# Loading value pairs, query weights and mixer input weights by one transfer of 56 to 64 KB per partition instead of two

## Chip, cores and metric

The kernel runs on one core of one Trainium2 chip. The metric is device time in microseconds (us); the lower the better. A measured time is the median of a few executions. A profile is one more execution, and its *span* is 1.3 to 1.4 us shorter than the measured time of the same execution. Times inside a profile are counted from the start of its span.

## What is computed

One decode step of attention with a cache of 65,536 positions, mixed by a gate with a small gated MLP. The inputs are bf16.

```python
q = x @ wq                                # 32 heads of 128, from a row of 1024
scores = q · k_cache * Dh**-0.5           # 4 kv heads, 65,536 keys each, 8 q heads per kv head
o = softmax(scores) · v_cache
a = o @ wo
z = gelu(B_x @ w_in); z1, z2 = halves     # 1024 -> 3584
b = (z1 * (w_sp * layernorm(z2) + b_sp)) @ w_out
out = g * a + (1 - g) * b                 # g = sigmoid(sum(x * gate_w))
```

The two caches are 67 MB each, the weights some 28 MB: 162 MB must be read once, for little arithmetic.

## The kernel before

Everything that is loaded goes through one list, `stream`, in a fixed order. A block of K or V is 16,384 positions of one head group: 4 MB, 32 KB in each of 128 partitions. The K blocks use a ring of three slots. The value blocks come in pairs, and there is **one** pair buffer, `VB`, which the query and mixer weights use before.

```python
SUB = 16384                               # elements of bf16: 32 KB per partition
...
load([("wq", 0)], rows(A_wq, 0, 8), VB)
load_k(0)
load_k(1)
load([("win", 0)], rows(B_w_in, 0, 8), VB)
load_k(2)
load_k(3)
load([("wout", 0)], rows(B_w_out, 0, 14), VB)
for i in range(6):
    load_k(2 * i + 4)
    load_v2(2 * i)                        # one pair: v(2i), v(2i+1), into VB
    load_k(2 * i + 5)
load_v2(12)
load([("v", 14)], kv(A_v_cache, 14), kring())
load([("v", 15)], kv(A_v_cache, 15), kring())
# ... then the output weights wo
```

`issue()` turns list entries into transfers. A transfer is recorded as soon as the program's order allows, and on the chip it waits until the readers of the slots that it overwrites are done. Every transfer has its own completion semaphore, and a reader waits for the transfers that wrote its slots.

```python
def issue():
    while issued[0] < len(stream):
        ...
        for c in range(0, w, SUB):        # at most 32 KB per partition in one transfer
            m = min(SUB, w - c)
            P("SP", lambda e, ...: e.dma_start(arena[:, o:o + m], src),
              w=[("slot", x) for x in grains(off + c, m)], dma="s%d" % grains(off + c, m)[0])
        issued[0] += 1
...
def pv_piece(n):                          # value product n, TensorE
    sl, keys = use(("v", n))              # keys: the slots of v(n) alone
    ...
    P("PE", f, r=[("ptsb", n % 2)] + keys, w=["ob"])
    done(("v", n))                        # frees the slots of v(n); issues what can be issued
```

The main loop scores K block `2i+4`, then does the two value products `2i` and `2i+1`, then scores K block `2i+5`. The query projection (`wqs, keys = use(("wq", 0))`) and the mixer projection name the slots of the whole tensor, so both halves must have landed before their first matmul.

## Time and profile before

| | before |
|---|---|
| measured time | 383.79 us (383.66 to 383.85, 3 runs) |
| span of the profile | 382.3 us |
| moved | 162 MB, 424 GB/s over the span |
| PE / DVE busy | 61% / 55% |

From the profile page of the kernel before: the DMA and clock rows of the table of 40 slices (each digit is tenths of a slice), the packet total, and the row of the main DMA queue with its packets, its MB and its share of 16 engines' span.

```profile
PEclk9996998689979599959898998786979988778695
DMA  9999999999999999999999999999999999999995
GB/s 384 439 435 425 423 417 435 439 436 433 439 425 418 432 430 439 439 432 432 429 420 429 435 439 434 429 435 426 422 432 437 435 432 429 439 425 420 423 425 220
DMA packets 6246, 162.16 MB, mean 424 GB/s; under 512 B 728, under 2 KB 732, under 8 KB 988
q1 hardware_dynamic: 6200, 162.01, 98.8%
```

The DMA engines were busy for nine tenths or more of every slice but the last. The kernel is bound by its stream of transfers. No computing engine can make it faster.

The end of the main loop: this is TensorE's timeline there, then the issues on the SP queue in the same stretch (columns: start, duration, engine, line, operation; in brackets, the idle time before and what ended it). `obt` is written by the value products: the first `scp` row ends the score block before, the next row is the start of product 10, the row with the bracket the start of product 11.

```profile
305.29 0.38 PE L248 MATMUL scp<-arena 128*128 128x512 bf16 x1
305.60 0.41 PE L246 MATMUL obt<-arena 128*64 128x512 bf16 x2
...
308.86 0.38 PE L248 MATMUL obt<-arena 128*64 128x512 bf16 x2
311.40 0.41 PE L246 MATMUL obt<-arena 128*64 128x512 bf16 x2 [2.16 <-DMA arena<-in_A_v_cache_dram]
...
316.32 0.41 PE L248 MATMUL obt<-arena 128*64 128x512 bf16 x2
```

```profile
309.28 8.77 SPq L365 DMA_DIRECT2D arena<-in_A_v_cache_dram  x4
```

Product 10 ran at once, on the half of the pair that had long landed. Its end released half of the pair buffer, and at 309.28 the next value transfer was in the queue. Product 11 waited for its half until 311.40.

The last view of before is the list of waits: how long TensorE waited for value blocks in all, how often, and the longest.

```profile
PE obt L246 <- DMA arena<-in_A_v_cache_dram: 12.4, 5, 6.1
```

### The profile page before, as it was taken

The page shows a single profiled execution, that of the slowest core. Times are in us where ns is not written, and L with a number is a line of the kernel's source. Part 1 is how long each engine was busy: PE and PEld are TensorE (multiplying, and loading weights), DVE is VectorE, ACT ScalarE, POOL GpSimd, SP SyncE. Part 2 cuts the span into 40 slices and gives each one's busy share as a digit, 9 for nine tenths or more (in the row PEclk, how much of TensorE's full clock was granted, in tenths as well). Part 3 has the DMA queues.
Part 4 walks back from the last instruction along what each step waited for, and adds up shares of the span by engine and source line. Part 5 has one row for each costly group of instructions (what it writes and reads, how often), then busy time and mean ns, then how long its engine had stood idle before and what let it go on. Part 6 is the DMA issues. An engine that isn't in the chain of part 4 may idle for free.

```text
span 382.3 us, 2522 instructions
## 1 busy us (share of the span) xinstructions
PE 234.6 (61%) x1375; PEld 56.9 (15%) x785; DVE 211.7 (55%) x229; ACT 25.3 (7%) x39; POOL 1.5 (0%) x8
## 2 busy tenths in 40 slices
PE   0055754286687578545793777377938673849344
PEld 0011111111121111101120112012201121112121
DVE  6116952785781698067935980579448914842020
ACT  1000000102030001000210010001200100031000
POOL 1000000000000000000000000000000000000000
PEclk9996998689979599959898998786979988778695
DMA  9999999999999999999999999999999999999995
GB/s 384 439 435 425 423 417 435 439 436 433 439 425 418 432 430 439 439 432 432 429 420 429 435 439 434 429 435 426 422 432 437 435 432 429 439 425 420 423 425 220
DMA packets 6246, 162.16 MB, mean 424 GB/s; under 512 B 728, under 2 KB 732, under 8 KB 988
## 3 DMA queue, kind: packets, MB, share of 16 engines
q1 hardware_dynamic: 6200, 162.01, 98.8%
q8 instruction: 8, 0.13, 0.1%
q14 instruction: 2, 0.02, 0.0%
q10 hardware_dynamic: 36, 0.00, 0.0%
HBM read 162.01 MB, written 0.00 MB: 424 GB/s over the span
## 4 chain that ended last, share of the span: by engine, by line
DMA 61%; PE 19%; DVE 18%; SPq 1%; ACT 1%; issue 1%
DMA arena<-in_A_k_cache_dram 33%; DVE arena L476 13%; DMA arena<-in_B_w_in_dram 8%; DMA arena<-in_A_wo_dram 7%; DMA arena<-in_B_w_out_dram 6%; PE obt L246 6%; DMA arena<-in_A_wq_dram 6%; PE obt L248 5%; PE scp L246 4%; PE scp L248 4%; DVE arena L493 1%; SPq L365 1%; DVE arena L514 1%; DVE arena L464 1%; DVE arena L549 0%
## 5 line engine op out<-in xcount | busy, mean ns | idle before, releaser
L476 DVE STREAM_TRANSPOSE arena<-arena 128x2048 f32<-128x2048 f32 x64 | 145.5, 2295 | 84.5 <-DMA arena<-in_A_k_cache_dram 71.9
L246 PE MATMUL scp<-arena 128*128 128x512 bf16 x256 | 112.5, 439 | 83.4 <-DVE arena L476 61.0
L248 PE MATMUL scp<-arena 128*128 128x512 bf16 x256 | 111.0, 434 | 0.0
L246 PE MATMUL obt<-arena 128*64 128x512 bf16 (+2 forms) x334 | 64.6, 428 | 30.6 <-DMA arena<-in_A_v_cache_dram 12.4
L248 PE MATMUL obt<-arena 128*64 128x512 bf16 (+2 forms) x334 | 64.1, 424 | 0.0
L246 PEld LDWEIGHTS scp<-arena 128*128 128x128 bf16 x256 | 27.5, 107 | 192.2 <-DVE arena L476 93.8
L509 ACT ACTIVATE arena<-arena 128x1024 bf16<-128x1024 f32 x16 | 18.4, 1148 | 237.5 <-DVE arena L505 127.4
L246 PEld LDWEIGHTS obt<-arena 128*64 128x64 bf16 (+1 forms) x334 | 19.4, 116 | 86.6 <-issue 79.1
L493 DVE TENSOR_SCALAR_CACHE_REDUCE arena<-scp 128x1024 f32<-128x1024 f32 x16 | 19.3, 1205 | 9.3 <-PE scp L248 9.3
L514 DVE STREAM_TRANSPOSE arena<-arena 128x1024 bf16<-128x1024 bf16 x16 | 19.4, 1214 | 9.0 <-PE obt L248 6.4
L706 PE MATMUL fbt<-arena 128*1 128x256 bf16 x128 | 6.2, 339 | 5.9 <-DMA arena<-in_A_wo_dram 5.7
L539 DVE RECIPROCAL arena<-mbt 128x1 f32<-128x1 f32 x4 | 0.6, 139 | 14.0 <-PE mbt L535 14.0
L441 DVE CAST arena<-obt 97x1024 bf16<-97x1024 f32 x1 | 1.2, 1224 | 11.5 <-PE obt L248 11.5
L712 DVE CAST arena<-fbt 97x256 bf16<-97x256 f32 x1 | 0.4, 425 | 11.3 <-PE fbt L706 11.3
L588 DVE COPY arena<-obt 128x896 f32<-128x896 f32 x1 | 1.1, 1093 | 9.1 <-PE obt L248 9.1
L464 DVE COPY arena<-arena 32x32 bf16<-32x32 bf16 x16 | 2.7, 166 | 6.2 <-PE scp L248 6.0
L407 PE MATMUL scp<-arena 8*128 8x1 bf16 x8 | 0.6, 197 | 8.4 <-DVE arena L402 8.4
L706 PEld LDWEIGHTS fbt<-arena 128*1 128x1 bf16 x128 | 2.8, 93 | 8.8 <-DMA arena<-in_A_wo_dram 6.7
L595 ACT ACTIVATE arena<-arena 128x28 f32<-128x28 f32 x1 | 0.2, 226 | 52.4 <-DVE arena L594 52.4
L549 DVE SCALAR_TENSOR_TENSOR arena<-obt,arena 128x512 bf16<-128x512 f32 x4 | 3.0, 751 | 0.1
L601 PE MATMUL mbt<-arena 128*128 128x1 f32 x2 | 0.4, 260 | 4.3 <-DVE arena L600 4.3
L509 ACT ACTIVATION_READ_ACCUMULATOR arena<-arena 128x1 f32 x16 | 3.0, 186 | 0.0
(88 smaller groups left out, 47.0 us busy)
## 6 DMA issues: line engine op xcount, KB each, us to landing
arena<-in_A_k_cache_dram SPq DMA_DIRECT2D x16, 4096.0 KB, 38.4
arena<-in_A_v_cache_dram SPq DMA_DIRECT2D x16, 4096.0 KB, 31.1
arena<-in_A_wq_dram SPq DMA_DIRECT2D x2, 4096.0 KB, 16.8
arena<-in_A_wo_dram SPq DMA_DIRECT2D x3, 2048.0 KB, 22.6
arena<-in_B_w_in_dram SPq DMA_DIRECT2D x1, 4096.0 KB, 25.2
arena<-in_B_w_out_dram SPq DMA_DIRECT2D x1, 3584.0 KB, 23.1
arena<-in_B_w_in_dram SPq DMA_DIRECT2D x1, 3072.0 KB, 32.2
arena<-in_A_wo_dram SPq DMA_DIRECT2D x1, 1024.0 KB, 26.5
```

The source lines that it names most:

```text
L246: return e.matmul(*a, **kw)
L248: one = e.matmul(*a, **kw).ins
L365: P("SP", lambda e, o=OFF["RING"] + off + c, m=m, src=src[:, c:c + m]: e.dma_start(arena[:, o:o + m], src), w=[("slot", x) for x in grains ...
L441: P("DVE", lambda e: e.tensor_copy(psb[0:97, :], ob[0:97, :]), w=["psb", "ob"])
L464: P("DVE", lambda e, pb=pb: e.tensor_copy(vw(qpad, 24 + 32 * pb, [[QP, 4], [1, 8]], 32 * pb, 32), vw(qall, 8 * g, [[32, 4], [1, 8]], 32 * ...
L476: P("DVE", lambda e: e.transpose(ktb(i).bitcast(F32), sl[:, 4096 * p:4096 * (p + 1)].bitcast(F32)), r=keys[2 * p:2 * p + 2], w=[("kt", i % ...
L493: P("DVE", lambda e: e.tensor_scalar(scs(n), sc_ps(n), 0.0, None, op0=ALU.add, op1=ALU.max, accum_out=maxc[:, n:n + 1]), w=[("sc", n % NSC ...
L509: P("ACT", lambda e: e.activation(psb, scs(n), ACTF.Exp, bias=gcol(n // NP, K_NB), scale=SCALE, accum_out=lp[:, n:n + 1]), r=[("sc", n % N ...
L514: P("DVE", lambda e: e.transpose(ptsb(n), psb), r=["psb"], w=[("ptsb", n % 2)])
L549: P("DVE", lambda e: e.scalar_tensor_tensor(osc, ob[:, 512:1024], gcol(g, K_FB), osc, op0=ALU.mult, op1=ALU.add), r=[("fh", g, 1), "psb"], ...
L588: P("DVE", lambda e: e.tensor_copy(vw(zr, 0, [[FB4, 2], [32, FC], [1, 32]]), vw(ob, 0, [[512, 2], [1, FC], [FC, 32]])), w=[KZR, "ob"])
L706: ins = e.matmul(fb[32 * q:32 * q + 1, 0:QW], ovec[:, 8 * i + c:8 * i + c + 1], sl[:, o:o + QW], start=False, stop=(i == 3 and c == 7), ti ...
```

## The change

The intent: fewer and larger transfers, so fewer packets with their fixed costs, and fewer semaphores. The Trainium skill points in this direction in "DMA: Bandwidth & Descriptors", section "Rules for kernel authors": for full bandwidth use 128 partitions and at least 1 MiB per transfer, and coalesce small transfers. Here the transfers were already 3 to 4 MB.

```diff
-            for c in range(0, w, SUB):
-                m = min(SUB, w - c)
+            for c in range(0, w, 2 * SUB):
+                m = min(2 * SUB, w - c)
```

Seven value pairs, the query weights (64 KB per partition) and the mixer input weights (56 KB) become one transfer each. The order of instructions on PE, DVE, ACT and POOL does not change.

## The prediction

> **What bounds the kernel now.** The DMA stream. In the slice table the 16 DMA engines read 9 tenths or more in every slice but the last; the hardware queue's packets fill 98.8% of 16 engines' span, 162 MB at a mean of 424 GB/s. In the packet records the engines are never idle together from the first packet (1.0 us after the first issue) to 379.1 us of the 382.3 us span. PE (61%) and DVE (55%) have room. So only two things can change the time: how long packets take, and whether the queue runs dry.
>
> **Packets (removed).** A 4 KB packet takes 159 ns, 8 KB 312, 16 KB 614, 32 KB 1216: about 37.6 ns per KB plus 10 to 12 ns per packet. The Trainium skill ("DMA: Bandwidth & Descriptors", "Why small descriptors are slow") names such a fixed cost per packet; at 32 KB the trace leaves 1% of it. The change merges nine pairs of transfers (query weights, mixer input weights, seven value pairs), each saving 8 packets per engine: 72 x 11 ns = 0.8 us, an estimate from those durations, with 64 KB packets of about 2.42 us.
>
> **Landings (moved).** Instruction order on PE, DVE and ACT is the same. The query and mixer projections already wait for both halves before their first matmul, so their merges move nothing. The value products do change: each waited for its half; the first of a pair will wait for the whole 8 MB, some 9.7 us later. Both products then run back to back, and the next value pair, which reuses the single pair buffer, is issued after both (before, its first half went after the first product).
>
> For most pairs that is harmless: two K blocks (19.5 us of work) stand in the queue behind the pair. Pair (2,3) would be released some 3 us later than 159.4 us, with the queue filled until 175.0. Pairs (4,5) and (8,9) hardly move.
>
> **The one place on the critical path**: pair (10,11) lands at 311.3 us and only block K15 is queued behind it, done at 318.9 (first engine) to 321.0 (last). Before, product 10 ran from 305.6 to 309.2 and released half the pair at 309.3, so the queue never ran dry. After, product 10 starts at about 310.7. A product takes 3.5 us at full granted clock, and 5.2 as product 11 ran at 311.4, because PE is granted half clock after idling. I expect both to end near 320 us, and first packets 1.0 to 1.2 us after the issue (the first issue of the trace shows 1.0), at about 321.1. The slowest engine would have gone on at 320.2: a bubble of about 1 us on it, 2 to 3 us on the others. Everything behind (last value blocks, output weights, tail of 2.8 us) shifts with it but has slack: the output weights are issued 10 us before the queue ends.
>
> **Sum**: -0.8 + 1.0 = +0.2 us: predicted 384.0 us, range 382.9 to 386.0. Chances: faster by over 2% 0.02, within 2% 0.94, slower by over 2% 0.04.
>
> **Right or wrong in the profile**: 64 KB packets near 2.42 us and 1,152 fewer data packets; PE waiting longer for the value cache; no first product before its pair lands; one dip of the DMA share near 320 us and none elsewhere; last output weights landing within 1.5 us of 379.5.
>
> **What would make it wrong**: large packets slower, or split into small ones; full PE clock after pair (10,11) (no bubble, about 383.1) or half clock throughout (3 us more); another pair running the queue dry; the late value pair delaying the final products past the output weights.

## The result, and the profile after

| | before | after |
|---|---|---|
| measured time | 383.80 us (4 runs) | 386.91 us (386.25 to 387.32, 4 runs) |
| ratio | | 1.0082, 95% interval 1.0067 to 1.0096 |
| span | 382.3 us | 386.0 us |
| PE's waits for value blocks | 12.4 us | 35.2 us |

A ratio is the mean time of one kernel's fast runs over that of the other's of the same rounds, so it is not quite the ratio of the medians above. The change costs 0.8%: within 2%, but 0.9 us outside the predicted range.

The page of the kernel after:

```profile
PEclk9997996589999898799696996899969968959695
DMA  9989999999999999999999999999999998989994
GB/s 435 435 380 435 430 437 429 429 434 440 435 418 435 452 430 407 421 469 435 394 433 472 435 397 433 469 435 402 428 460 445 404 394 336 435 379 435 423 421 194
DMA packets 4951, 162.16 MB, mean 420 GB/s; under 512 B 585, under 2 KB 589, under 8 KB 845
q1 hardware_dynamic: 4904, 162.01, 97.8%
```

The same bytes moved in 1,295 fewer packets (9 merged transfers x (128 data packets + 16 semaphore writes) = 1,296). The rate swings between 379 and 472 GB/s from slice to slice where it was level before. I take these swings for an effect of counting whole packets of 2.4 us into slices of 9.7 us: in the packet records no engine idles there, and the run with 32 KB packets and the same waits, below, does not have them. Slice 34, with 336 GB/s, is different. A window wider than a packet shows it. The rows are the windows of 10 us around the end of block K15, for before and then for after (columns: window, length, busy us and count of PE, PEld, DVE, ACT, POOL, then granted clock, DMA share and GB/s):

```profile
316.00:326.00 10.00, 3.67 (x17) 0.88 (x8) 4.92 (x6) 0.00 (x0) 0.00 (x0) 0.81 1.03 442
```

```profile
316.00:326.00 10.00, 7.88 (x52) 1.85 (x25) 5.28 (x7) 0.00 (x0) 0.00 (x0) 0.84 0.76 298
```

The DMA share falls from 1.03 to 0.76. (A share over 1 arises at the edges of a window, so it is good to a few per cent only.) The packet records (one row per packet in the packed trace, with its start, length and size; a row does not name its engine, so two rows are taken for one engine's when one starts as the other ends) give the loss closely: from 317.95 to 322.49 us, fewer than 16 engines were at work, and 2.97 us of each engine's time were lost on the mean. From 2 to 375 us there is no other such place in the profile of after, and there is none at all in that of before.

Why the queue was empty is in TensorE's timeline and the SP queue's, of the kernel after:

```profile
305.11 0.38 PE L248 MATMUL scp<-arena 128*128 128x512 bf16 x1
310.97 0.64 PE L246 MATMUL obt<-arena 128*64 128x512 bf16 x2 [5.49 <-DMA arena<-in_A_v_cache_dram]
311.40 0.64 PE L248 MATMUL obt<-arena 128*64 128x512 bf16 x2
...
315.67 0.61 PE L248 MATMUL obt<-arena 128*64 128x512 bf16 x2
316.10 0.40 PE L246 MATMUL obt<-arena 128*64 128x512 bf16 x2
...
320.21 0.38 PE L248 MATMUL obt<-arena 128*64 128x512 bf16 x2
```

```profile
320.63 1.28 SPq L365 DMA_DIRECT2D arena<-in_A_v_cache_dram  x3
```

Product 10 now waits 5.49 us for the whole pair. Then both products run one after the other, the first 12 steps at 0.43 us from start to start, the later ones at 0.22: half clock first, then full. The pair buffer is free only at 320.6 us. The only block queued behind the pair, K15, had by then ended on all engines (317.9 to 320.2 us in the packet records), and the next packets start at 321.6. The view of waits and the chain of work that ended last tell the same: the chain of after goes through this wait, from one value pair to its products to the next value pair.

```profile
PE obt L246 <- DMA arena<-in_A_v_cache_dram: 35.2, 9, 6.1
```

```profile
279.33 31.60 DMA arena<-in_A_v_cache_dram
...
310.97 0.64 PE obt L246 x2
...
320.63 21.82 DMA arena<-in_A_v_cache_dram
```

Finally, a ledger from the completion semaphores: when the last of the 16 engines finished each transfer, with the time of the first engine in brackets (us).

| landed | before | after | shift of the last |
|---|---|---|---|
| K15 | 320.98 (318.88) | 320.63 (318.47) | -0.35 |
| pair (12,13), whole | 340.40 (338.30) | 342.46 (341.86) | +2.06 |
| V14 | 350.12 (348.02) | 353.50 (351.57) | +3.38 |
| V15 | 359.84 (357.72) | 363.21 (361.29) | +3.37 |
| last output weights | 379.50 (377.45) | 383.17 (381.30) | +3.67 |
| output written | 382.29 | 385.97 | +3.68 |

The loss comes in two steps. The first is at the dry spot. The second, 1.3 us, comes one transfer later, where the queue was full. Note the brackets: in the first row the 16 engines are 2.2 us apart, after the dry spot 0.6 us, and one transfer later 1.9 us again.

### The profile page after: what moved, and what is told of

It is laid out like the page before. It is cut to its first block, busy times and chain, and to the rows that moved or that the text cites. A ratio compares the mean times of both kernels' runs of the same rounds, so it can differ in the third digit from the quotient of the medians.

```text
span 386.0 us, 2504 instructions
## 1 busy us (share of the span) xinstructions
PE 229.2 (59%) x1375; PEld 55.5 (14%) x785; DVE 211.3 (55%) x229; ACT 25.3 (7%) x39; POOL 1.5 (0%) x8
## 4 chain that ended last, share of the span: by engine, by line
DMA 79%; PE 19%; SPq 0%; issue 0%; ACTq 0%; DVE 0%
DMA arena<-in_A_v_cache_dram 53%; PE obt L246 9%; PE obt L248 9%; DMA arena<-in_B_w_in_dram 8%; DMA arena<-in_A_wo_dram 8%; DMA arena<-in_B_w_out_dram 6%; DMA arena<-in_B_b_sp_dram 5%; SPq L365 0%; ACTq L271 0%; PE fbt L706 0%; PE scp L419 0%; DVE arena L712 0%; DVE arena L418 0%; DVE arena L417 0%; PE mbt L412 0%
## 5 line engine op out<-in xcount | busy, mean ns | idle before, releaser
L246 PE MATMUL scp<-arena 128*128 128x512 bf16 x256 | 107.3, 419 | 72.6 <-DVE arena L476 60.6
L248 PE MATMUL scp<-arena 128*128 128x512 bf16 x256 | 106.1, 414 | 0.0
L246 PE MATMUL obt<-arena 128*64 128x512 bf16 (+2 forms) x334 | 65.8, 439 | 42.1 <-DMA arena<-in_A_v_cache_dram 35.2
L248 PE MATMUL obt<-arena 128*64 128x512 bf16 (+2 forms) x334 | 65.3, 436 | 0.0
L246 PEld LDWEIGHTS scp<-arena 128*128 128x128 bf16 x256 | 26.5, 104 | 175.4 <-DVE arena L476 93.4
L514 DVE STREAM_TRANSPOSE arena<-arena 128x1024 bf16<-128x1024 bf16 x16 | 19.4, 1213 | 11.3 <-PE obt L248 8.7
```

Source lines behind the costliest of these rows:

```text
L246: return e.matmul(*a, **kw)
L248: one = e.matmul(*a, **kw).ins
L514: P("DVE", lambda e: e.transpose(ptsb(n), psb), r=["psb"], w=[("ptsb", n % 2)])
```

## The experiments

The theory, "dry queue": all of the loss is that the queue runs empty once, because pair (12,13) is issued too late. This needs two things together: product 10 waits for the whole pair, and the next pair is issued only after both products. Rivals: large transfers cost something themselves; or the late start of product 10 alone is the cause. Every run was timed in 5 rounds beside the kernel before; the tables give the medians.

### The weights alone

From the kernel before:

```diff
-            for c in range(0, w, SUB):
-                m = min(SUB, w - c)
+            st = 2 * SUB if keys[0][0] in ("wq", "win") else SUB
+            for c in range(0, w, st):
+                m = min(st, w - c)
```

> Only the query and mixer input weights are merged; the value pairs stay split. Theory 'dry queue' (all of the loss comes from the queue running empty before value pair (12,13)): no dry spot, time 383.6 to 383.8 us, ratio 0.999 to 1.000 of the kernel before. Rival 'large transfers cost something themselves' (64 KB packets, or their slow first packets): a part of the 3.1 us appears here, at least 0.5 us, so 384.3 us or more.

Measured: 383.62 us against 383.73, ratio 0.9997 (0.9984 to 1.0010); no dry spot. The merged weights are not the cause, and 64 KB packets at the start of the kernel cost nothing that the times show.

### Value pair (10,11) split again

From the kernel after:

```diff
-            for c in range(0, w, 2 * SUB):
-                m = min(2 * SUB, w - c)
+            st = SUB if keys[0] == ("v", 10) else 2 * SUB
+            for c in range(0, w, st):
+                m = min(st, w - c)
```

> The changed kernel, but value pair (10,11) is two transfers again; pair (12,13) stays one, issued after both products. Dry queue: product 10 runs on its own half before the pair is complete, only product 11 stands before the issue at about 316.8 us, and first packets follow 1.0 us later, just before the queue empties at about 318.2 to 320.4 us: dry spot at most 0.3 us mean, time 383.1 to 383.6 us. Large transfers cost something themselves: 386.4 us or more, since six of seven value pairs and both weights are still merged.

Measured: 383.09 us against 383.73, ratio 0.9984 (0.9971 to 0.9996); the next pair was issued at 314.44 us, and the packet records show no dry spot:

```profile
314.44 1.28 SPq L366 DMA_DIRECT2D arena<-in_A_v_cache_dram  x3
```

That is 2.4 us earlier than expected. Product 11 came after an idle time of only 1.39 us and took 3.6 us, at full clock. Eight of the nine merges are still there. One pair decides.

### Value pair (12,13) split again

From the kernel after: the same edit, with `("v", 12)` in place of `("v", 10)`.

> The changed kernel, but value pair (12,13) is two transfers again; pair (10,11) stays one. Dry queue: product 10 still starts only at about 310.7 us, but the first half of the next pair is issued when it ends, near 316.5 us, with first packets near 317.5, before the queue empties: dry spot at most 0.4 us mean, time 383.1 to 383.9 us. If the late start of product 10 alone were the cause (rival), the time stays at 386.4 us or more.

Measured: 383.18 us against 383.73, ratio 0.9990 (0.9977 to 1.0002), no dry spot. TensorE's timeline still has the late start of product 10, with a wait of 4.91 us:

```profile
310.96 0.64 PE L246 MATMUL obt<-arena 128*64 128x512 bf16 x2 [4.91 <-DMA arena<-in_A_v_cache_dram]
```

Its end at about 316 us now released half of the buffer:

```profile
316.07 4.74 SPq L366 DMA_DIRECT2D arena<-in_A_v_cache_dram  x4
```

So the late product alone costs nothing that the times show, and neither does the release of the pair as a whole alone (the run above). It takes both.

### Both waits with the old transfers

From the kernel before: no transfer is merged, but each product of a pair names the slots of the whole pair.

```diff
         sl, keys = use(("v", n))
+        if n < 14:
+            keys = use(("v", n - n % 2))[1] + use(("v", n - n % 2 + 1))[1]
```

> All transfers as in the kernel before (32 KB packets), but each value product of a pair waits for both halves, and so the next pair is issued after both products. Dry queue: the same dry spot as in the changed kernel, 2.5 to 3.5 us mean near 318 to 322.5 us, time 386.5 to 388.0 us. Large transfers cost something themselves: no or little loss, 383.8 to 384.8 us.

Measured: 387.75 us (4 runs) against 383.73, ratio 1.0102 (1.0087 to 1.0118). The packet records have one dry spot, 318.4 to 323.1 us, 3.29 us lost. The same window as above:

```profile
316.00:326.00 10.00, 8.20 (x53) 2.17 (x26) 4.83 (x6) 0.00 (x0) 0.00 (x0) 0.84 0.69 275
```

The whole loss is here with 32 KB packets: it is made by the waits and not by the size of packets. It is larger than the changed kernel's by about 0.9 us. That fits with what the larger packets save and with a dry spot that was 0.3 us longer; the two were not taken apart.

### Another block queued behind the pair

From the kernel after: all merges and waits stay, only the order of the queue changes. V14 goes to a K ring slot that is free by then.

```diff
-    load_v2(12)
     load([("v", 14)], kv(A_v_cache, 14), kring())
+    load_v2(12)
```

> The changed kernel with all its merges and waits, but value block 14 stands in the queue ahead of pair (12,13), so that two blocks (about 19.4 us) instead of one cover the pair's products. Dry queue: pair (12,13) is issued at about 320.6 us as before, but the queue is filled until about 328 to 330 us: no dry spot, 383.0 to 383.6 us. If the large transfers or the wait for the pair cost time by themselves: 386.4 us or more.

Measured: 383.19 us against 383.66, ratio 0.9990 (0.9976 to 1.0004); no dry spot, although pair (12,13) is issued at 320.26 us, nearly as late as in the changed kernel (320.63). The issue, and the window:

```profile
320.26 0.80 SPq L365 DMA_DIRECT2D arena<-in_A_v_cache_dram  x2
```

```profile
316.00:326.00 10.00, 6.50 (x51) 1.71 (x25) 5.24 (x7) 0.00 (x0) 0.00 (x0) 1.00 1.01 433
```

The wait for the pair is harmless while the queue holds two blocks behind it.

### The second step of the loss: engines drifting apart

The ledger's second step (+1.3 us, with a full queue) needs its own reason. In the packet records of after, one 16 KB instruction packet at 346.75 us took 0.97 us, and the data packet that starts as it ends 1.71 us instead of 1.22: one engine lost 1.46 us, and a transfer is done only when its last engine is. The page of before has 8 such packets (queue q8, "instruction"), spread over the span. The theory, "skew": early in the run such packets put some engine 2 us behind, and later ones that fall on other engines cost nothing, for those have 2 us in hand. A dry spot lets the late engine catch up, so the next instruction packet costs time again.

The completion semaphores of before fit this. The 16 engines end each large transfer within 0.6 us of each other up to 41.2 us. In the next transfer, after the first 16 KB instruction packet (44.3 us), they end 1.9 us apart, and they stay 1.9 to 2.2 us apart to the end: none of the seven later packets widens that by as much as 0.1 us. The run with both waits and the old packets has the second step too: its pair (12,13) lands 2.60 us later than before, V14 3.88 us later.

To test it, the late instruction packets were removed, by taking TensorE instructions out of both kernels. The arithmetic is incomplete (the comparison with the reference passed all the same, within its tolerance).

```diff
-            for fe in range(4):
+            for fe in (range(4) if n < 15 else (0, 3)):
...
-            for i in range(16):
+            for i in (range(16) if 9 <= n <= 11 else (0, 15)):
...
-                for q in range(4):
+                for q in (range(4) if (i, c) == (3, 7) else [c % 4]):
```

Control, from the kernel before:

> Control for the next run; the result is wrong on purpose. The kernel before with many TensorE instructions taken out (value products 0 to 8 and 12 to 15 of 2 steps instead of 16, fewer in the last score block and the output projection), so that the two instruction fetches at 345 and 372 us no longer happen. All transfers and their order are the same. Both theories of the next run: 383.2 to 383.9 us, since the queue never runs dry and one engine is already 2 us behind from the fetches near 44 and 59 us.

The same edit on the kernel after:

> The changed kernel with the same instructions taken out; wrong on purpose. Theory 'skew': a dry spot lines the 16 engines up again, and then the next instruction fetch (346.8 us) puts one engine 1.5 to 2 us behind once more, so that the spot costs the idle time of the early engines and not of the late one. Without late fetches: only the late engine's idle time, that is 1.6 us less than in the full kernel, 1.5 to 2.3 us over the trimmed kernel before; the last output weights land within 1 us of each other over the 16 engines. Rival 'the dry spot costs its mean idle time plus the restart whatever the fetches': still 3 to 3.7 us over the trimmed kernel before.

Measured: the control 383.77 us, ratio 1.0001 (0.9989 to 1.0014); the trimmed changed kernel 385.71 us, ratio 1.0055 (1.0042 to 1.0067). Both have no instruction packet after 316 us. The trimmed changed kernel has its dry spot (2.87 us lost) and is 1.9 us slower than the control, inside what "skew" expected and well below 3 us. After the dry spot its engines stay together: V14 lands from 351.37 to 352.10, 0.7 us apart, against 1.9 us in the full kernel. And the second step is gone: against the control the pair lands 1.97 us late and V14 2.02 us late. At the very end they are 1.1 us apart, a little over the 1 us expected.

The mechanism is shown; its worth in time is less sure. The changed kernel's nine runs in all (here and in the last experiment) have a mean of 386.66 us, the five trimmed ones 385.80: a difference of 0.9 us and not the 1.6 expected (the two sets were not timed beside each other). Part of the gap can be read in the profile: between the landings of the last three transfers (1, 0.5 and 0.5 MB) 3.13 us passed, against 2.77 in the full changed kernel and 2.50 in the control. What makes small packets slower there was not tried.

### TensorE kept at full clock

In the changed kernel the two products took 9.6 us (310.97 to 320.59), of which the first 5.1 at half clock. The Trainium skill, "TensorE: Matmul & The Clock Gate", section "Part 1: The HAM clock gate", says that an idle window of about 3.4 us puts the array to half clock, that a busy one releases it, and that the windows run freely. The trace agrees: 5.5 us of idling, then half clock until 316.1. The window need not be wholly idle, though: in the kernel before, product 11 came after 2.16 us of idling, and from 311.9 to 315.3 us the granted clock was a half all the same; in the 3.5 us before that TensorE had been busy for 1.34 us. From the kernel after:

```diff
+        if i == 5:
+            def warm(e):
+                for j in range(25):
+                    ins = mm(e, j > 0, sc_ps(15)[:, 0:512], qpad[:, 0:128], qpad[:, 0:512], start=True, stop=True, ...)
+                return ins
+            P("PE", warm, r=["qpad"], w=[KSC(15)])
         pv_piece(2 * i)
         pv_piece(2 * i + 1)
```

> The changed kernel with 25 useless matmuls (128x512, into the score bank that block 15 will overwrite) put ahead of value product 10, so that TensorE is busy instead of idle from about 305.5 to 310.9 us while it waits for pair (10,11). Theory 'half clock after the wait': the two products then run at full granted clock, about 7.0 us instead of 9.3, the next pair is issued near 318.1 us instead of 320.6, first packets near 319.2: dry spot about 0.5 to 1.2 us mean instead of 3.0, time 384.0 to 385.3 us. Rival 'the clock has no part in it': products take 9 us as before, 386.4 us or more.

> The changed kernel itself, unaltered, on the same chip as the run beside it. Both theories: 386.3 to 387.3 us, one dry spot near 318 to 322.5 us.

Measured: 384.75 us with the useless matmuls (ratio 1.0024, 1.0010 to 1.0037), and 386.35 us for the changed kernel again (1.0069, 1.0055 to 1.0083), against 383.80. TensorE's timeline with the useless matmuls:

```profile
310.85 0.41 PE L246 MATMUL obt<-arena 128*64 128x512 bf16 x2 [0.18 <-DMA arena<-in_A_v_cache_dram]
...
317.56 0.38 PE L248 MATMUL obt<-arena 128*64 128x512 bf16 x2
```

```profile
317.98 1.28 SPq L365 DMA_DIRECT2D arena<-in_A_v_cache_dram  x3
```

The products end 2.7 us earlier, the next pair is issued at 317.98 instead of 320.63, and the loss in the dry spot falls from 2.97 to 0.69 us per engine. Of the 2.6 us that the changed kernel costs beside it, 1.6 came from the half clock. In the profile of the repeated changed kernel, half clock ended at 314.9 us instead of 316.1; there the pair was issued at 320.01, and 2.20 us were lost. The nine runs of the changed kernel spread over 1.25 us. That the moment at which half clock ends makes this spread is likely from the two profiles and not shown: the kernel before spread over 0.21 and 0.25 us in two sets of nine runs, but over 1.12 in the third, by one run.

## Why the prediction was right or wrong

- **The bound, and the only place where time could be lost**: right. The queue ran dry at one place, behind K15, for the reason given; splitting either of two pairs or one more block behind them removes it.
- **The merged weights move nothing**: right (383.62 against 383.73 us).
- **Packets**: right. 64 KB packets take 2.42 us (median 2.421), and 1,295 packets went away. The saving, predicted as 0.8 us, was 0.64, 0.55 and 0.47 us in the three runs with eight or nine merges and no dry spot; only the first is clear of noise.
- **Products 10 and 11 end near 320 us**: right (issue at 320.63, 320.01 when repeated); that half clock sets it was shown by taking it away. To hit 320 that closely was in part luck, since half clock ended at 316.1 us in one profile and at 314.9 in the other.
- **The other pairs**: harmless, as predicted. Only the lateness of pair (2,3) was too small: the pair after it was issued at 164.4 us, 5 us and not 3 later than 159.4, while the queue was filled until 175.
- **The step that failed** is the term "+1.0" in the sum, from "a bubble of about 1 us on it, 2 to 3 us on the others". The mechanism was right, the size was off: with the old packets this term measures 4.0 us (387.75 against 383.73); with the larger ones 3.1 and 2.6 us are left after their saving. Three things were left out or too small:
  - The slowest engine was idle at least 1.4 us and not 1.0 (the last K15 packet ended at 320.2, new ones started from 321.6).
  - The restart: the 16 first packets after the dry spot took 3.12 us on the mean instead of 2.42, so 0.7 us more. The first packets of the kernel show the same (1.6 to 2.1 us for 32 KB instead of 1.22); it could have been read from the trace of before.
  - The cost was counted on the latest engine, as if it stayed the latest. After the dry spot the engines were level, and the next instruction packet put one behind again: +1.3 us in the ledger. The early engines' idle time was not free. The profile nearly adds up, with the small transfers at the end (+0.3) and the earlier landing of K15 (-0.35): 1.4 + 0.7 + 1.3 + 0.3 - 0.35 = 3.35, of 3.7 us. The rest, 0.3 us, is not accounted for.
- **Last output weights within 1.5 us of 379.5**: wrong for these reasons (383.17).

## What to carry to other kernels

When transfers that fill one buffer are merged, ask what the first half's early landing did: here it let a product run early and hand half of the buffer back early. Compare the time from landing to the next issue (two products, at the clock that TensorE has after waiting) with the work queued behind: one 4 MB block (9.7 us) was too little, two were enough. Here a dry spot in a bound queue cost more than the idle time of the latest engine, so count the early engines' idle time and the restart.

## What the Trainium skill lacked or had wrong

- "DMA: Bandwidth & Descriptors", "Rules for kernel authors", advises coalescing small transfers into large ones. From 4 to 8 MB this was worth 0.5 to 0.6 us of 384, barely clear of noise, and the coarser completion cost 3 to 4 us. That section lacks the caution that a transfer is also the unit of waiting and of release.
- The same page gives about 600 ns for the first byte of a transfer issued from SP ("Latency and other measured facts"), and lacks from where this is counted. Here it was 1.0 us from the start of the issuing instruction to the first packet, both at the start of the kernel and after the dry spot (320.63 to 321.59), but 0.6 us from that instruction's end (0.39 to 1.01, 320.96 to 321.59).
- No page that I read has the cost of restarting a drained queue: the first packet of each engine took 0.7 us longer on the mean with 64 KB packets, 0.5 us with 32 KB.
- No page that I read has the cost of instruction packets for a bound queue: a 16 KB packet took 0.9 to 1.1 us on one engine and slowed the next data packet by about 0.5 us. In the kernel before, the engines were 1.9 us apart from the first such packet on; that this is absorbed until a dry spot levels them was shown by the trimmed kernels.
- "TensorE: Matmul & The Clock Gate", "Part 1: The HAM clock gate", lacks how busy a window may be and still count as idle: in the kernel before, 1.34 us of work in 3.5 us were followed by half clock.
- "CRC Debugging" ("Comparing the Two Runs") puts instruction refills on queue 14. The profile here counts 8 instruction packets of 16 KB on queue 8, beside those on queue 14.
